# Second product of an expert mixture: six matmuls per visit to an accumulator instead of three

## The chip, the core and the metric

The kernel runs on one core of a Trainium2 chip. The metric is device microseconds (us) of one execution. TensorE (PE) multiplies, with a weight loader of its own (PEld); VectorE (DVE), ScalarE (ACT) and GpSimd (POOL) do the elementwise work; SyncE (SP) issues most DMAs.

## The reference, cut to what matters

A gated linear attention gives 3072 rows of 384. A first mixture, `(a * b @ w3) @ w_out`, maps them to 3072 x 384 again, and a second mixture of four experts follows:

```
p = domain_probs / domain_probs.sum(-1)
out = 0
for e in range(4):
    h = relu(x @ w1[e])              # 3072 x 384 by 384 x 1024
    out += p[:, e:e+1] * (h @ w2[e]) # 3072 x 1024 by 1024 x 384
```

The change is in this last loop alone.

## The kernel before

Every fp32 product is made of three matmuls on operands split in a high and a low part (`mm3`: high by high, low by high, high by low; lines L86, L87 and L88). I call these three matmuls a **visit**. All visits here have 128x128 weights and 384 moving columns.

The second mixture runs in 32 **passes**, numbered 0 to 31: four experts `e`, by four tiles `t` of 768 tokens, by two halves `k` of the 1024 columns of the hidden layer. An even pass has k = 0, an odd one k = 1.

**First product.** A pass forms `x @ w1[e]` for 512 hidden columns and 768 tokens by a scheme with 20 products where plain tiling has 24. The table `PARTS` lists them in 19 **groups**, 0 to 18. A group is one visit (group 10 has two) to one of two PSUM banks of the pool `pho` (the tile is called hps), followed by **steps**, which add or subtract the bank to or from slots of `raw_x`. So the first visit of group g+2 must wait until the last step of group g that reads the bank is over. The steps are numbered 0 to 27 in `PARTS`; steps 0 to 2 are copies on ACT (L1292), the rest additions on DVE (L1294). Steps 6, 15, 17 and 23 read `raw_x` alone; the others read a bank. Some of what the following text needs: group 12 has steps 16 and 17, group 13 step 18, group 14 steps 19 and 20, group 15 steps 21, 22 and 23, group 16 step 24, group 17 steps 25 and 26, group 18 step 27.

**h tiles.** Eight entries "h" of `PARTS` (at groups 6, 8, 10, 11, 14, 15, 17 and 18) turn a finished slot into an **h tile**, a block f of 128 hidden columns for one half of the 768 tokens: two ACT operations, L1275 for the high part and L1276, then one POOL operation for the low part, L1277. Before the change nine buffers are given out in turn.

**Second product.** `h @ w2[e]` has six PSUM accumulators per token tile (the tile is called ops), m = 0 to 5, one for each 128 tokens: m = 0 to 2 for the first half, 3 to 5 for the second. Each takes eight visits: four blocks f in the even pass, four in the odd. The function `second` makes one visit. The visits of a pass are done during the next pass: `blocks` lists the 24 of them, and after each group g the table `SHARE[g]` says how many of them follow. All instructions keep this order on their engine; nothing reorders them. Before the change the list goes h tile by h tile, as they were made, three accumulators for each.

When an accumulator has had its eighth visit, `second` puts one **eviction** on DVE (L1244 for the first expert, L1246 for the others): scale by the expert's share and add to the running sum `ac`, which is then stored. The eighth visits come in the even passes.

In the six passes 7, 8, 15, 16, 23 and 24 DVE also makes the low parts of the next expert's first weights (L1024, behind the steps of groups 3, 5, 7 and 9).

Of the kernel before, what the change touches and what calls it, by code (L numbers as in the profile page):

```python
# [26 lines left out]
HT = 384  # L27
# [42 lines left out]
W_STEPS = ((0, 0, 6), (0, 6, 12), (1, 0, 6), (0, 12, 16), (1, 6, 12), (0, 16, 20), (1, 12, 16), (1, 16, 20))  # L70
SHARE = (2, 1, 1, 1, 0, 1, 2, 1, 1, 1, 1, 1, 1, 1, 1, 2, 2, 2, 2)
SIGN = {"+": ALU.add, "-": ALU.subtract}
# [405 lines left out]
def gated_attention_moe_kernel(tc, qT, kT, aT, vP, w1, w2, w3T, wo, probs, ew, out):  # L478
# [4 lines left out]
    with tc.manual_schedule(), root:  # L483
# [491 lines left out]
        def x_open():  # L975
            for _ in range(4):
                x = wtile([128, 4, 2, HT], F32R, "xo")
                xslots.extend(x[:, n] for n in range(4))
            w = xtp.tile([128, 4 * NP * TT], F32R, tag="xt", name="wa")
            wslots.append(w[:, :2 * NW * 128].rearrange("p (s n c) -> p s n c", s=2, n=NW))  # L980

        def x_sum(eng, t, dst, x, y, op):
# [237 lines left out]
        made = [(f, h) for _, steps in PARTS for _, f, h, op in steps if op == "h"]  # L1220
        turned = [made[2], made[0], made[1]] + made[3:]
        accs = {}
        h_at = {}
        done_h = [0]
        last_use = {o: g for g, (parts, _) in enumerate(PARTS) for _, o in parts}

        def second(i, f, m):
            e, t, k = octs[i]
            half = m // 3
            mine = [b for b, h in (made if k or not i else turned) if h == half]  # L1230
            if (e, t, m) not in accs:
# [4 lines left out]
            last = k == KO - 1 and f == mine[-1]  # L1236
            mm3(nc, ps, hh[:, 0, tok], hh[:, 1, tok], w[:, 0], w[:, 1], k == 0 and f == mine[0], last)
            if not last:
                return
# [16 lines left out]
        def blocks(i):  # L1256
            k = octs[i][2]
            return [(i, f, 3 * h + m) for f, h in (made if k or not i else turned) for m in range(3)]

# [7 lines left out]
        def combine(i, ps, steps, where, left):  # L1267

            for v, x, y, op in steps:
                if op == "h":  # L1270
                    free.append(where.pop(v))
                    s = tmp[:, free[-1]]
                    hh = h_at[i, x, y] = hslots[done_h[0] % len(hslots)]
                    done_h[0] += 1
                    A.activation(out=hh[:, 0], in_=s, func=ACTF.Relu)  # L1275
# [21 lines left out]
        for i, (e, t, k) in enumerate(octs):  # L1297
# [4 lines left out]
            for g, (parts, steps) in enumerate(PARTS):  # L1302
# [7 lines left out]
                combine(i, ps, steps, where, left)  # L1310
                for _ in range(SHARE[g] if i > 1 else g != 4 if i else g > 12):
                    if todo:
                        second(*todo.pop(0))
# [82 lines left out]
```

## Time and profile before

| | |
|---|---|
| median of 3 runs | 1196.36 us (1196.05 to 1198.81) |
| profiled execution, its own time | 1197.35 us |
| its span, first to last instruction | 1195.5 us |
| PE busy | 1167.1 us, 98% |
| DVE busy | 829.2 us, 69% |
| ACT busy | 627.4 us, 52% |
| POOL busy | 445.1 us, 37% |
| passes 0 to 31 | from 440.1 us to 1189.6 us of the span |

The rows of the timeline give a start, a duration, the engine, the line, the tile written, an arrow and the tiles read; in brackets stands idle time of the engine just before, and what ended it. Rows with x2 or more merge neighbours: their time runs from the first start to the last end. DVE and PE are pipelined, so a row may start before the one ahead of it has ended. A matmul lasts 0.34 us in the record, but the next starts some 0.175 us after it.

### The profile page before, as it was taken

How to read it: one execution, taken by the hardware profiler on the slowest of the kernel's cores; microseconds unless marked ns; L12 is line 12 of the kernel's file. 1: busy time of each engine (PE TensorE's matmuls, PEld its weight loads, DVE VectorE, ACT ScalarE, POOL GpSimd, SP SyncE). 2: the span in 40 equal slices, each digit the busy share in tenths (PEclk: the TensorE clock that was granted, in tenths of full speed). 3: DMA queues.
4: the chain of work that ended last, by engine and by line, in shares of the span. 5: the costliest groups of instructions: out<-in, count | busy, mean ns of one | idle time of the engine just before them, and what ended most of it. 6: DMA issues, size and time to landing. Idle time of an engine off the chain costs nothing.

```text
span 1195.5 us, 24960 instructions
## 1 busy us (share of the span) xinstructions
PE 1167.1 (98%) x9186; PEld 1149.3 (96%) x9186; DVE 829.2 (69%) x1513; ACT 627.4 (52%) x1238; POOL 445.1 (37%) x517
## 2 busy tenths in 40 slices
PE   5899999999999999999999999999999999999997
PEld 4799999999999999999999999999999999999997
DVE  8898788966665856667677656667666587576563
ACT  4565555554544445454666655666565545444432
POOL 2133321010000006776744434744433655433332
PEclk9899999999999999999999999999999999999999
DMA  8756675555775696478576595695784863753821
GB/s 318 223 171 188 211 216 200 173 166 192 272 284 177 243 337 226 168 304 292 208 288 225 199 330 203 244 347 178 275 303 156 307 244 127 290 176 142 291 81 43
DMA packets 131171, 269.54 MB, mean 225 GB/s; under 512 B 17376, under 2 KB 64992, under 8 KB 131040
## 3 DMA queue, kind: packets, MB, share of 16 engines
q1 hardware_dynamic: 130176, 266.67, 63.8%
q8 instruction: 75, 1.23, 0.4%
q10 hardware_dynamic: 864, 1.18, 0.3%
q14 instruction: 56, 0.46, 0.1%
HBM read 207.24 MB, written 58.20 MB: 222 GB/s over the span
## 4 chain that ended last, share of the span: by engine, by line
PE 95%; DVE 3%; DMA 1%; issue 0%; POOL 0%; SPq 0%; ACT 0%; DVEq 0%; POOLq 0%
PE ops L87 11%; PE ops L86 11%; PE ops L88 11%; PE hps L86 9%; PE hps L87 9%; PE hps L88 9%; PE abps L86 6%; PE abps L87 6%; PE abps L88 6%; PE xps L86 3%; PE xps L88 3%; PE xps L87 3%; PE yps L673 2%; PE yps L691 1%; PE wps L86 1%; PE wps L88 1%
## 5 line engine op out<-in xcount | busy, mean ns | idle before, releaser
L1294 DVE TENSOR_TENSOR raw_x<-hps,raw_x 128x384 f32<-128x384 f32 x416 | 226.4, 554 | 212.3 <-PE hps L88 197.2
L1277 POOL TENSOR_TENSOR ht<-raw_x,ht 128x384 fp32r<-128x384 f32 x227 | 238.1, 1051 | 274.5 <-ACT raw_x L1276 222.2
L1275 ACT ACTIVATE ht<-raw_x 128x384 fp32r<-128x384 f32 x227 | 118.6, 523 | 228.3 <-DVE raw_x L1294 215.9
L87 PE MATMUL ops<-wb,ht 128*128 128x384 f32 x681 | 231.5, 340 | 0.0
L86 PE MATMUL ops<-wb,ht 128*128 128x384 f32 x681 | 230.8, 339 | 0.0
L88 PE MATMUL ops<-wb,ht 128*128 128x384 f32 x681 | 230.6, 339 | 0.0
L86 PE MATMUL hps<-xo,wa 128*128 128x384 f32 x640 | 217.8, 340 | 2.5 <-DVE raw_x L1294 1.2
L87 PE MATMUL hps<-xo,wa 128*128 128x384 f32 x640 | 215.5, 337 | 0.0
L88 PE MATMUL hps<-xo,wa 128*128 128x384 f32 x640 | 215.1, 336 | 0.0
L1294 DVE TENSOR_TENSOR raw_x<-raw_x,hps 128x384 f32<-128x384 f32 x256 | 136.5, 549 | 25.5 <-PE hps L88 25.1
L1276 ACT ACTIVATE raw_x<-raw_x 128x384 f32<-128x384 f32 x256 | 134.7, 526 | 8.1
L86 PEld LDWEIGHTS hps<-xo,wa 128*128 128x128 f32 x640 | 120.2, 188 | 8.4 <-DVE raw_x L1294 6.0
L86 PEld LDWEIGHTS ops<-wb,ht 128*128 128x128 f32 x681 | 128.0, 188 | 0.0
L88 PEld LDWEIGHTS ops<-wb,ht 128*128 128x128 f32 x681 | 127.9, 188 | 0.0
L87 PEld LDWEIGHTS ops<-wb,ht 128*128 128x128 f32 x681 | 127.5, 187 | 0.0
L87 PEld LDWEIGHTS hps<-xo,wa 128*128 128x128 f32 x640 | 120.2, 188 | 0.0
L88 PEld LDWEIGHTS hps<-xo,wa 128*128 128x128 f32 x640 | 120.1, 188 | 0.0
L1294 DVE TENSOR_TENSOR raw_x<-raw_x 128x384 f32<-128x384 f32 x128 | 88.6, 692 | 4.4
L698 POOL MEMSET Z<- 128x1 f32 x18 | 1.8, 98 | 191.7 <-PE yps L673 191.7
L1277 POOL TENSOR_TENSOR ho<-raw_x,ho 128x384 fp32r<-128x384 f32 x29 | 30.7, 1060 | 105.0 <-DMA xo<-kept 71.4
L86 PE MATMUL abps<-xt,w2h 128*128 128x384 f32 x192 | 66.0, 344 | 0.0
L86 PE MATMUL abps<-xt,w1h 128*128 128x384 f32 x192 | 65.9, 343 | 0.0
(136 smaller groups left out, 2224.2 us busy)
## 6 DMA issues: line engine op xcount, KB each, us to landing
xo<-kept SPq DMA_DIRECT2D x272, 384.0 KB, 6.4
kept<-ac SPq DMA_DIRECT2D x45, 384.0 KB, 2.9
partial<-ac SPq DMA_DIRECT2D x72, 192.0 KB, 1.9
ac<-partial SPq DMA_DIRECT2D x72, 192.0 KB, 6.4
spilled<-g_sb SPq DMA_DIRECT2D x64, 192.0 KB, 2.3
gg<-spilled SPq DMA_DIRECT2D x64, 192.0 KB, 3.3
c_raw<-in_w3T_dram SPq DMA_DIRECT2D x16, 512.0 KB, 4.1
raw_x<-in_w3T_dram SPq DMA_DIRECT2D x8, 1024.0 KB, 7.0
```

Of the source, the lines that this page charges most:

```text
L86: nc.tensor.matmul(out=ps, lhsT=lh, rhs=rh, start=first, stop=False)
L87: nc.tensor.matmul(out=ps, lhsT=ll, rhs=rh, start=False, stop=False)
L88: nc.tensor.matmul(out=ps, lhsT=lh, rhs=rl, start=False, stop=last)
L673: PE.matmul(out=r["y"][rows, p, t], lhsT=Z[rows, p], rhs=r["q"][rows, p, half], start=p == 0, stop=False)
L691: PE.matmul(out=r["y"][rows, p, t], lhsT=v[half, p, g], rhs=r["s"][half, g, p], start=first and t == 0 and p == 0, stop=p == NP - 1)
L698: G.memset(r["Zh"][:, NP - 1, 63:], 0.0)
L1275: A.activation(out=hh[:, 0], in_=s, func=ACTF.Relu)
L1276: A.activation(out=s, in_=s, func=ACTF.Relu)
L1277: G.tensor_tensor(out=hh[:, 1], in0=s, in1=f32(hh[:, 0]), op=ALU.subtract)
L1294: V.tensor_tensor(out=tmp[:, s], in0=ins[0], in1=ins[1], op=SIGN[op])
```

## The change

- `blocks` gives the 24 visits by **pairs**: the first two blocks f of the first half, the first two of the second half, then the last two of each. Within a pair, for each of the three accumulators both blocks follow each other, so that six matmuls in a row go to one accumulator.
- `SHARE` has only 0 and 2, so the visits stand in twos; groups 0, 2, 4, 6, 9, 10 and 13 have none. Passes 0 and 1 get numbers of their own in the same manner.
- The order of blocks is the same in even and odd passes (`turned` is gone).
- A tenth h tile comes from the unused end of the tile `xt` that holds first weights (in order's rows it has the name wa). Buffers are no longer given out in turn: `second` puts one back in the list when its third visit is issued.

```diff
--- before.py
+++ after.py
@@ -68,7 +68,7 @@
     (5, 3, 5, "-"), (5, 12, 0, "x"), (1, 13, 0, "x"), (7, 7, 3, "-"), (7, 14, 0, "x"), (8, 8, 6, "-"),
     (8, 15, 0, "x"), (2, 2, 6, "+"), (2, 16, 0, "x"))
 W_STEPS = ((0, 0, 6), (0, 6, 12), (1, 0, 6), (0, 12, 16), (1, 6, 12), (0, 16, 20), (1, 12, 16), (1, 16, 20))
-SHARE = (2, 1, 1, 1, 0, 1, 2, 1, 1, 1, 1, 1, 1, 1, 1, 2, 2, 2, 2)
+SHARE = (0, 2, 0, 2, 0, 2, 0, 2, 2, 0, 0, 2, 2, 0, 2, 2, 2, 2, 2)
 SIGN = {"+": ALU.add, "-": ALU.subtract}
 NW, NX, NT = 20, 17, 9
 
@@ -978,6 +978,7 @@
                 xslots.extend(x[:, n] for n in range(4))
             w = xtp.tile([128, 4 * NP * TT], F32R, tag="xt", name="wa")
             wslots.append(w[:, :2 * NW * 128].rearrange("p (s n c) -> p s n c", s=2, n=NW))
+            hslots.append(w[:, 2 * NW * 128:2 * NW * 128 + 2 * HT].rearrange("p (s n) -> p s n", s=2))
 
         def x_sum(eng, t, dst, x, y, op):
             r = raw_x[t % 2]
@@ -1218,16 +1219,16 @@
             job(split_b(e, 1), *((i0 + 1, g) for g in range(3, 11)))
 
         made = [(f, h) for _, steps in PARTS for _, f, h, op in steps if op == "h"]
-        turned = [made[2], made[0], made[1]] + made[3:]
+        by_half = [[b for b in made if b[1] == h] for h in range(2)]
+        pairs = [by_half[h][n:n + 2] for n in (0, 2) for h in range(2)]
         accs = {}
         h_at = {}
-        done_h = [0]
         last_use = {o: g for g, (parts, _) in enumerate(PARTS) for _, o in parts}
 
         def second(i, f, m):
             e, t, k = octs[i]
             half = m // 3
-            mine = [b for b, h in (made if k or not i else turned) if h == half]
+            mine = [b for b, _ in by_half[half]]
             if (e, t, m) not in accs:
                 accs[e, t, m] = poo.tile([128, 512], F32, tag="o", name="ops")[:, :DM]
             ps = accs[e, t, m]
@@ -1235,6 +1236,8 @@
             tok = slice(m % 3 * 128, (m % 3 + 1) * 128)
             last = k == KO - 1 and f == mine[-1]
             mm3(nc, ps, hh[:, 0, tok], hh[:, 1, tok], w[:, 0], w[:, 1], k == 0 and f == mine[0], last)
+            if m % 3 == 2:
+                hslots.append(h_at.pop((i, f, half)))
             if not last:
                 return
             b, c = chunks[t * 6 + m]
@@ -1254,8 +1257,7 @@
             nc.sync.dma_start(out=f32(tiles["ac"][:, m // 2, m % 2]), in_=partial[b * NCH + c])
 
         def blocks(i):
-            k = octs[i][2]
-            return [(i, f, 3 * h + m) for f, h in (made if k or not i else turned) for m in range(3)]
+            return [(i, f, 3 * h + m) for pair in pairs for m in range(3) for f, h in pair]
 
         uses = {}
         for _, steps in PARTS:
@@ -1270,8 +1272,7 @@
                 if op == "h":
                     free.append(where.pop(v))
                     s = tmp[:, free[-1]]
-                    hh = h_at[i, x, y] = hslots[done_h[0] % len(hslots)]
-                    done_h[0] += 1
+                    hh = h_at[i, x, y] = hslots.pop(0)
                     A.activation(out=hh[:, 0], in_=s, func=ACTF.Relu)
                     A.activation(out=s, in_=s, func=ACTF.Relu)
                     G.tensor_tensor(out=hh[:, 1], in0=s, in1=f32(hh[:, 0]), op=ALU.subtract)
@@ -1308,7 +1309,7 @@
                     if k == KO - 1 and last_use[o] == g and n + 1 < E * NT2:
                         x_load((t + 1) % NT2, o)
                 combine(i, ps, steps, where, left)
-                for _ in range(SHARE[g] if i > 1 else g != 4 if i else g > 12):
+                for _ in range(SHARE[g] if i > 1 else 2 * (g % 2 == 0 and g < 18) if i else 2 * (g in (13, 15, 17))):
                     if todo:
                         second(*todo.pop(0))
                 for gen in jobs.pop((i, g), ()):
```

What stands in a row, at two places. The first is PE at the start of pass 13, an odd pass, with hps the banks of the first product and ops the accumulators; the number is that of the tile. Before:

```order
L86 MATMUL hps_8911<-xo_5298,wa_5732 128x384
L87 MATMUL hps_8911<-xo_5298,wa_5732 128x384
L88 MATMUL hps_8911<-xo_5298,wa_5732 128x384
L86 MATMUL ops_8917<-wb_7890,ht_5892 128x384
L87 MATMUL ops_8917<-wb_7890,ht_5892 128x384
L88 MATMUL ops_8917<-wb_7890,ht_5892 128x384
L86 MATMUL ops_8921<-wb_7890,ht_5892 128x384
L87 MATMUL ops_8921<-wb_7890,ht_5892 128x384
L88 MATMUL ops_8921<-wb_7890,ht_5892 128x384
L86 MATMUL hps_8926<-xo_5728,wa_5732 128x384
L87 MATMUL hps_8926<-xo_5728,wa_5732 128x384
L88 MATMUL hps_8926<-xo_5728,wa_5732 128x384
```

After:

```order
L86 MATMUL hps_8911<-xo_5298,wa_5732 128x384
L87 MATMUL hps_8911<-xo_5298,wa_5732 128x384
L88 MATMUL hps_8911<-xo_5298,wa_5732 128x384
L86 MATMUL hps_8918<-xo_5728,wa_5732 128x384
L87 MATMUL hps_8918<-xo_5728,wa_5732 128x384
L88 MATMUL hps_8918<-xo_5728,wa_5732 128x384
L86 MATMUL ops_8924<-wb_7889,ht_5891 128x384
L87 MATMUL ops_8924<-wb_7889,ht_5891 128x384
L88 MATMUL ops_8924<-wb_7889,ht_5891 128x384
L86 MATMUL ops_8924<-wb_7743,ht_5891 128x384
L87 MATMUL ops_8924<-wb_7743,ht_5891 128x384
L88 MATMUL ops_8924<-wb_7743,ht_5891 128x384
```

The visit of group 1 (the second hps) stood behind two visits to accumulators; it now follows that of group 0, and the two visits behind it go to one accumulator.

The second place is DVE in pass 12, an even pass, from step 18 (before) and from the first eviction (after); ac marks the evictions. Before:

```order
L1294 TENSOR_TENSOR raw_x_3840<-hps,raw_x_3840 128x384 x2
L1294 TENSOR_TENSOR raw_x_3840<-raw_x_3840,hps 128x384
L1294 TENSOR_TENSOR raw_x_3840<-hps,raw_x_3840 128x384 x2
L1294 TENSOR_TENSOR raw_x_3840<-raw_x_3840 128x384
L1294 TENSOR_TENSOR raw_x_3840<-hps,raw_x_3840 128x384
L1246 SCALAR_TENSOR_TENSOR ac<-ops,p_sb,ac 128x384 x2
L1294 TENSOR_TENSOR raw_x_3840<-hps,raw_x_3840 128x384
L1294 TENSOR_TENSOR raw_x_3840<-raw_x_3840,hps 128x384
L1246 SCALAR_TENSOR_TENSOR ac<-ops,p_sb,ac 128x384 x2
L1294 TENSOR_TENSOR raw_x_3840<-hps,raw_x_3840 128x384
L1246 SCALAR_TENSOR_TENSOR ac<-ops,p_sb,ac 128x384 x2
```

After:

```order
L1249 SCALAR_TENSOR_TENSOR ac<-ops,p_sb,ac 128x384
L1295 TENSOR_TENSOR raw_x_3840<-hps,raw_x_3840 128x384 x2
L1295 TENSOR_TENSOR raw_x_3840<-raw_x_3840,hps 128x384
L1249 SCALAR_TENSOR_TENSOR ac<-ops,p_sb,ac 128x384
L1295 TENSOR_TENSOR raw_x_3840<-hps,raw_x_3840 128x384 x2
L1295 TENSOR_TENSOR raw_x_3840<-raw_x_3840 128x384
L1249 SCALAR_TENSOR_TENSOR ac<-ops,p_sb,ac 128x384
L1295 TENSOR_TENSOR raw_x_3840<-hps,raw_x_3840 128x384
L1249 SCALAR_TENSOR_TENSOR ac<-ops,p_sb,ac 128x384
L1295 TENSOR_TENSOR raw_x_3840<-hps,raw_x_3840 128x384
L1295 TENSOR_TENSOR raw_x_3840<-raw_x_3840,hps 128x384
L1249 SCALAR_TENSOR_TENSOR ac<-ops,p_sb,ac 128x384
L1295 TENSOR_TENSOR raw_x_3840<-hps,raw_x_3840 128x384
```

The six evictions stood in twos behind steps 24, 26 and 27. Now one stands ahead of step 18, one each between 20 and 21 and between 23 and 24, one ahead of and one behind steps 25 and 26, and the sixth behind step 27.

## Rows read from the trace of the kernel before

**Rows 1.** Busy by stretch, passes 0 to 31: each engine's us, PEclk, DMA, GB/s
```profile
440.00:1195.50 755.50, 746.98 (x4226) 740.75 (x4226) 496.81 (x922) 399.48 (x746) 378.97 (x428) 1.00 0.63 228
```

**Rows 2.** Waits of PEld, 440 to 1195: us in total, times, longest
```profile
PEld hps L86 <- DVE raw_x L1294: 6.0, 16, 1.6
```

**Rows 3.** The same waits in 595 to 627, then in 782 to 814
```profile
PEld hps L86 <- DVE raw_x L1294: 1.2, 4, 0.3
...
PEld hps L86 <- DVE raw_x L1294: 1.1, 4, 0.3
```

**Rows 4.** Timeline of PE around one of these waits, pass 7, group 8
```profile
601.36 0.34 PE L88 MATMUL ops<-wb,ht 128*128 128x384 f32 x1
601.66 0.45 PE L86 MATMUL hps<-xo,wa 128*128 128x384 f32 x1
601.95 0.34 PE L87 MATMUL hps<-xo,wa 128*128 128x384 f32 x1
```

**Rows 5.** Timeline of DVE ahead of it: weights, then three steps
```profile
599.73 0.95 DVE L1024 TENSOR_TENSOR wa<-araw,wa 128x768 fp32r<-128x768 f32 x1
600.60 1.48 DVE L1294 TENSOR_TENSOR raw_x<-raw_x,hps 128x384 f32<-128x384 f32 x3
```

**Rows 6.** Timeline of PE: pass 12 starts, group 10 ends, pass 13 starts
```profile
709.28 0.34 PE L86 MATMUL hps<-xo,wa 128*128 128x384 f32 x1
...
721.22 0.33 PE L88 MATMUL hps<-xo,wa 128*128 128x384 f32 x1
...
732.48 0.34 PE L86 MATMUL hps<-xo,wa 128*128 128x384 f32 x1
```

**Rows 7.** DVE, pass 12: steps 12; 17; 18, 19; 20; 23; 26; evictions; 27
```profile
721.65 0.56 DVE L1294 TENSOR_TENSOR raw_x<-hps,raw_x 128x384 f32<-128x384 f32 x1 [1.07 <-PE hps L88]
...
724.30 1.11 DVE L1294 TENSOR_TENSOR raw_x<-raw_x 128x384 f32<-128x384 f32 x1
725.33 1.24 DVE L1294 TENSOR_TENSOR raw_x<-hps,raw_x 128x384 f32<-128x384 f32 x2
726.49 0.54 DVE L1294 TENSOR_TENSOR raw_x<-raw_x,hps 128x384 f32<-128x384 f32 x1
...
728.00 0.56 DVE L1294 TENSOR_TENSOR raw_x<-raw_x 128x384 f32<-128x384 f32 x1
...
730.51 0.55 DVE L1294 TENSOR_TENSOR raw_x<-raw_x,hps 128x384 f32<-128x384 f32 x1
730.97 1.14 DVE L1246 SCALAR_TENSOR_TENSOR ac<-ops,p_sb,ac 128x384 f32<-128x384 f32 x2
732.02 0.55 DVE L1294 TENSOR_TENSOR raw_x<-hps,raw_x 128x384 f32<-128x384 f32 x1
```

**Rows 8.** POOL, pass 12: low parts of the h tiles of steps 13 and 20
```profile
723.98 1.02 POOL L1277 TENSOR_TENSOR ht<-raw_x,ht 128x384 fp32r<-128x384 f32 x1 [2.19 <-ACT raw_x L1276]
...
728.36 1.08 POOL L1277 TENSOR_TENSOR ht<-raw_x,ht 128x384 fp32r<-128x384 f32 x1 [2.08 <-ACT raw_x L1276]
```

**Rows 9.** PE, first matmuls of visits: first mixture; last pass; first mixture again
```profile
256.86 0.34 PE L86 MATMUL xps<-gg,w3h 128*128 128x384 f32 x1
...
273.81 0.34 PE L86 MATMUL xps<-gg,w3h 128*128 128x384 f32 x1
...
1177.67 0.34 PE L86 MATMUL ops<-wb,ht 128*128 128x384 f32 x1
...
1187.74 0.34 PE L86 MATMUL ops<-wb,ht 128*128 128x384 f32 x1
...
282.28 0.34 PE L86 MATMUL xps<-gg,w3h 128*128 128x384 f32 x1
...
288.52 0.34 PE L86 MATMUL xps<-gg,w3h 128*128 128x384 f32 x1
```

**Rows 10.** The end: the six last evictions, and the issues of their stores
```profile
1186.35 3.27 DVE L1246 SCALAR_TENSOR_TENSOR ac<-ops,p_sb,ac 128x384 f32<-128x384 f32 x6 [10.57 <-PE ops L88]
...
1187.00 3.93 ACTq L1250 DMA_DIRECT2D out_dram<-ac  x6
```

## The prediction

> **What bounds the kernel now.** I read the busy times by stretch first. In the passes of the second mixture PE works 746.98 of 755.50 us at full granted clock, 1.00 [rows 1]. The count of matmuls does not change, so only two things can move the time: the distance from one matmul to the next, and PE's waits. The distance is even: pass 12 starts at 709.28 and pass 13 at 732.48 [rows 6], 23.20 us for 44 visits, 0.527 us each or 0.176 us a matmul. Then come the waits: only visits of the first product wait for DVE, 16 times and 6.0 us in all [rows 2], and no visit to an accumulator is in the list. So DVE's queue near such a wait is the next view, and what it collides with on POOL [rows 7, 8]. The end of the program is the third place.
>
> **Matmuls.** 384 changes of accumulator go. What one costs: in the first mixture 32 visits go 24 matmuls to a bank and take 273.81 - 256.86 = 16.95 us, 0.530 each; in the last pass 19 visits, each to another bank, take 1187.74 - 1177.67 = 10.07 us, 0.530 each [rows 9]. I take nothing for them. The Trainium skill ("TensorE: Matmul & The Clock Gate", section on psum-queue depth-cycling) says that cycling through PSUM banks can make TensorE idle briefly between groups, so that its clock falls. By that rule fewer changes would raise the clock; here it reads 1.00 already, so the sum would gain nothing by it either.
>
> **Waits that go.** In six passes DVE also makes weights. PE then waits twice in a pass for a bank, at groups 6 and 8: four times in two passes, 1.2 and 1.1 us of waits in the first two such stretches [rows 3]; the third reads like the first. What one costs PE: the distances 601.36 to 601.66 and to 601.95 are 0.30 and 0.29 instead of 0.176 [rows 4], 0.24 together, of which 0.11 is the slow first matmul after a wait. Twelve make 2.9 us. DVE was 0.95 us on weights just ahead, and three steps followed without a gap [rows 5]. Between groups 4 and 6 there now lie three visits instead of two, 0.53 us more than the 0.12 us that was missing: that wait goes. Between groups 6 and 8 there are three instead of four, so the other may stay: the saving lies between 6 x 0.24 = 1.4 and 2.9 us. I take 1.4, since DVE has the same work there.
>
> **A wait that comes.** I follow DVE through the even pass 12, with durations from its rows. From the end of a product to its step is 0.26 us (matmul at 721.22 [rows 6], plus 0.176; step 12 at 721.65 [rows 7]), and this is never what comes last below.
> - Step 17 reads `raw_x` alone. It began at 724.30 while POOL worked from 723.98 to 725.00 [rows 8], and ended at 725.41, 0.41 after POOL; step 18 began at 725.33 [rows 7]. After the change group 10 has one visit less ahead of it, so steps 12 to 17 and POOL's tile are all 0.53 us earlier. An eviction stands behind step 17 (0.53: two took 730.97 to 732.02 [rows 7]). Both cancel: step 18 is at 725.33 again, step 20 at 726.49.
> - From step 20 to step 23 it was 1.51 us (726.49 to 728.00). An eviction now stands between: step 23 begins at 728.53.
> - POOL's work on the h tile of step 20 stays at 728.36 [rows 8]. It began 0.36 us behind step 23; now it is 0.17 us ahead. Step 23, too, reads `raw_x` alone, so it waits as step 17 did: POOL takes 1.02 us to 729.38, step 23 ends at 729.79, and the next begins 0.08 before that, at 729.71.
> - Behind it are queued: eviction 729.71, step 24 at 730.24, eviction 730.71 (0.47 a step: three in 1.48 [rows 5]), step 25 at 731.24, step 26 at 731.71, eviction 732.17 (0.46 after it, as 730.51 to 730.97), step 27 at 732.70, over at 733.25. Before it began at 732.02 [rows 7].
> - Who waits: step 27 frees the bank for group 1 of pass 13. That visit used to have two visits to accumulators ahead of it; now it is next to group 0 and due at 732.48 + 0.53 = 733.01. PE resumes 0.04 us after a step's end (601.07 + 0.55 against 601.66 [rows 4, 5]), at 733.29: a wait of 0.28, with the slow matmul 0.11 about 0.39 us.
>
> There are 15 even passes with evictions (2 to 30). In pass 22 PE already waits, for the single matmul of the check of the inputs behind group 14; that lets DVE catch up. So 14 x 0.39 = 5.5 us. From both sides: if step 23 is only a little late, DVE is 0.37 us in hand and the cost is 0; with every link 0.05 us longer it is 0.45 x 15 = 6.8.
>
> How POOL and DVE collide matters here. Step 17's row shows a step that stands still until POOL is done. If the two shared at half speed instead, step 23 would end near 729.51 (0.85 us at half speed, then 0.13), the whole queue 0.28 earlier, and the wait would vanish. The Trainium skill ("SBUF — State Buffer", Who interferes with whom) calls it an exclusive lock on a shared port, held for a whole instruction by whichever starts first. The trace agrees (0.41 us after POOL's end), and by that rule the 0.17 us of lead decide.
>
> **Other edits.** Visits to accumulators wait for h tiles on nobody: every tile is made at least 13 groups before its first visit. The tenth buffer and the list take waits off ACT and POOL, which are not late; nothing. Stores follow evictions on SP's queue, now earlier in the pass; loads behind them have a pass of room; nothing. Passes 0 and 1 keep 6 and 18 visits, and DVE there sets when PE goes on: nothing, or 0.3 either way.
>
> **The end.** The last six evictions were done in one row to 1186.35 + 3.27 = 1189.62, and the six stores' issues reached 1187.00 + 3.93 = 1190.93 [rows 10], because evictions 0.53 apart outran issues of up to 0.65. Now an accumulator ends every 1.06 us, so only one issue is left behind the last eviction: its end moves to 1190.27 or earlier. That is 0.7 us. The rows do not show what the end of the span hangs on, so 0 to 0.9.
>
> **Sum.** Against the profiled execution (1197.35, span 1195.5): +5.5 - 1.4 - 0.7 = +3.4 us. That execution is 1.0 us above the median 1196.36; put on the median it gives 1199.8. Own range of this case: 0.25 x 14 - 2.9 - 0.9 = -0.3 to 6.8 - 1.4 = +5.4, 1196.1 to 1201.8. A change under 0.3% (3.6 us: 1192.8 to 1199.9) can't be told from none.
>
> **Rivals.**
> - *The new wait does not come.* If step 23 gets in ahead of POOL, step 27 is over by 732.4 and group 1 starts on time. For it: the margin is 0.17 us out of a chain of some ten links. Against it: times repeat closely from pass to pass in this stage, and POOL's lead comes from step 20 alone. It leaves -1.4 - 0.7 = -2.1, or -3.8 with the second wait gone: 1192.6 to 1194.3, the other side of my forecast. Chance 24%.
> - *More places open.* In the same chain step 24 ends at 730.79 and the visit of group 18 needs its bank at 730.89 (41 visits after 709.28): 0.1 us in hand; group 11 follows group 9 after two visits; ACT's copies for groups 0 to 2 stand behind the late step 27. In passes 2 to 6, 13, 14, 21 and 22 POOL has more work and more steps stand still. One more wait of 0.15 us in 30 passes adds 4.5 us to my sum: 1204. Chance 13%.
> - *The second visit of a pair runs faster.* The first mixture has stretches at 0.520 us a visit (282.28 to 288.52 is twelve visits [rows 9]) beside those at 0.530, with the same code. If the visits in pairs to one accumulator fell into that pace, 12 x 32 x 0.010 = 3.8 us would go: 1196.0 with the new wait, 1190.4 without. Nothing in the rows ties the pace to the bank. Chance 9%.
>
> **Chances.** My case has 54%: slower by over 0.3% in 23, within in 31. First rival: within 16, faster 8. Second: slower 13. Third: within 4, faster 5. So faster 13%, same 51%, slower 36%. The range runs from 1192.5 (some 9% below it, in the first and third rival) to 1203.8 (some 7% above it, in the second).
>
> **What would show it.** Right: in passes 12, 14 and so on step 23 takes over 1.1 us instead of 0.56 and starts just behind POOL; PE waits at group 1 of odd passes, on step 27; pairs of passes take 46.8 us instead of 46.40; the waits at group 6 of the six passes are gone; the last issue ends about 1 us nearer to the last matmul. Wrong: step 23 stays at 0.56, or the odd passes start on time, or the distance of matmuls inside a pair differs from 0.176 us: then the sum fails at that term.

## The result, and the profile after

The changed kernel takes 1207.34 us (median of 5 runs, 1206.26 to 1208.77) against 1196.36 us (5 runs, 1194.46 to 1198.81). The ratio is 1.0086, with a 95% interval of 1.0072 to 1.0101: it is slower by 0.7 to 1.0%. I forecast 1199.8 us, slower by 0.3%, and a range that ended at 1203.8; the sign was right and the size was not. Most of the 11 us are waits of PE: one kind that I had forecast (4.0 us), one that I had overlooked (3.0), and several in the first passes (4.0).

The profiled execution has a span of 1207.0 us, 11.4 us more than before. From the first matmul of pass 0 to the last one of the program it is 758.63 us instead of 748.53, which is 10.1 of the 11.4; 1.0 us lies behind the last matmul and 0.3 us ahead of pass 0, in code that the change does not touch.

From pass 0 to just behind the last matmul, by windows (microseconds, then busy time and count of PE, PEld, DVE, ACT and POOL, then PEclk, DMA share, GB/s; [rows 1] runs on to the end of the span, which adds 0.7 us of DVE):

```profile
440.40:1199.40 759.00, 752.65 (x4226) 738.81 (x4226) 516.92 (x921) 399.04 (x745) 378.48 (x428) 1.00 0.63 226
```

The matmuls are the same 4226 and the clock is 1.00 again. ACT and POOL work as long as before. DVE works some 20 us longer with the same instructions. Two groups of the list by line say which of them grew (behind the first bar stand busy time and mean ns of one; before, the first group read 88.6, 692 and the second 40.8, 611):

```profile
L1295 DVE TENSOR_TENSOR raw_x<-raw_x 128x384 f32<-128x384 f32 x128 | 105.1, 821 | 4.4
...
L1249 DVE SCALAR_TENSOR_TENSOR ac<-ops,p_sb,ac 128x384 f32<-128x384 f32 x72 | 43.8, 608 | 10.9 <-PE ops L88 10.9
```

One eviction takes what it did (its total rose by 3 us only because neighbours overlap less). The steps that read `raw_x` alone, which are 6, 15, 17 and 23, went from 692 to 821 ns on average: they stand still more often. What PE feels of it is in the waits of PEld, the answer to [rows 2]:

```profile
PEld hps L86 <- DVE raw_x L1295: 14.8, 37, 1.0
PEld hps L86 <- ACT raw_x L1293: 2.8, 4, 1.6
```

From 16 waits of 6.0 us to 37 of 14.8, and a second line that was 0.2 us before: waits for ACT's copies, steps 0 to 2.

To place them I took the distance between the starts of all neighbouring matmuls of the passes (the two small ones of the check of the inputs left out). Where it is over some 0.2 us, I summed what it has over 0.1755 us, the usual distance. This **excess** holds the wait and the slow first matmul after it. It is 6.3 us before and 16.6 us after:

| where | before | after | forecast of the difference | measured |
|---|---|---|---|---|
| group 1 of odd passes | 0 | 4.0 | +5.5 | +4.0 |
| the six weight passes | 2.8 | 4.5 | -1.4 | +1.7 |
| passes 0 to 6, without group 1 of 3 and 5 | 2.6 | 6.6 | 0 (passes 0 and 1: either way 0.3) | +4.0 |
| all the rest of the passes (20 and 22 above all) | 1.0 | 1.6 | 0 | +0.6 |
| behind the last matmul's start | 6.9 | 7.9 | -0.7 | +1.0 |

The distance itself did not move: its mean without waits is 175.75 ns before and 175.72 ns after.

**The wait that was forecast** is there, link by link. DVE in pass 12 of the changed kernel, which starts at 715.31: steps 20, eviction of m 1, steps 21 and 22, step 23, and, behind the left-out rows, step 27. Then POOL's h tile, then PE at the start of pass 13:

```profile
732.51 0.54 DVE L1295 TENSOR_TENSOR raw_x<-raw_x,hps 128x384 f32<-128x384 f32 x1
732.97 0.61 DVE L1249 SCALAR_TENSOR_TENSOR ac<-ops,p_sb,ac 128x384 f32<-128x384 f32 x1
733.50 1.01 DVE L1295 TENSOR_TENSOR raw_x<-hps,raw_x 128x384 f32<-128x384 f32 x2
734.55 1.26 DVE L1295 TENSOR_TENSOR raw_x<-raw_x 128x384 f32<-128x384 f32 x1
...
738.69 0.55 DVE L1295 TENSOR_TENSOR raw_x<-hps,raw_x 128x384 f32<-128x384 f32 x1
...
734.36 1.02 POOL L1278 TENSOR_TENSOR ht<-raw_x,ht 128x384 fp32r<-128x384 f32 x1 [2.58 <-ACT raw_x L1277]
...
738.89 0.34 PE L88 MATMUL hps<-xo,wa 128*128 128x384 f32 x1
739.29 0.45 PE L86 MATMUL hps<-xo,wa 128*128 128x384 f32 x1
739.58 0.34 PE L87 MATMUL hps<-xo,wa 128*128 128x384 f32 x1
```

Step 23 began 0.19 us behind POOL and ended at 735.81, 0.43 us after POOL's end at 735.38. Step 27 ended at 739.24, and PE went on at 739.29. The distances 0.40 and 0.29 are 0.34 us too long together; 0.39 were forecast.

**A wait that was not forecast** stands in the weight passes, at group 12. In pass 7 of the changed kernel, DVE makes the fourth low part of the weights and then the two steps that read the bank of group 10 (the second row and the first half of the third); POOL's h tile of the same time and PE at group 12 follow:

```profile
608.53 1.36 DVE L1025 TENSOR_TENSOR wa<-araw,wa 128x512 fp32r<-128x512 f32 x1
609.82 0.55 DVE L1295 TENSOR_TENSOR raw_x<-hps,raw_x 128x384 f32<-128x384 f32 x1
610.28 1.00 DVE L1295 TENSOR_TENSOR raw_x<-raw_x,hps 128x384 f32<-128x384 f32 x2
...
608.33 1.02 POOL L1278 TENSOR_TENSOR ht<-raw_x,ht 128x384 fp32r<-128x384 f32 x1 [0.51 <-ACT raw_x L1277]
...
610.30 0.34 PE L88 MATMUL ops<-wb,ho 128*128 128x384 f32 x1
610.88 0.45 PE L86 MATMUL hps<-xo,wa 128*128 128x384 f32 x1 [0.24 <-DVE raw_x L1295]
```

The weight instruction reads two operands from SBUF (`araw` and `wa`), as step 23 does, and it, too, stood still until POOL was done. In the kernel before the same instruction ran 0.32 us ahead of POOL's, took its 0.68 us, and POOL was the one to wait (1.25 us, and 1.02 when it runs alone):

```profile
604.02 0.68 DVE L1024 TENSOR_TENSOR wa<-araw,wa 128x512 fp32r<-128x512 f32 x1
...
604.34 1.25 POOL L1277 TENSOR_TENSOR ht<-raw_x,ht 128x384 fp32r<-128x384 f32 x1 [0.52 <-ACT raw_x L1276]
```

The order of the two turned because of the places. POOL's tile hangs on the product of group 8, the weight part stands behind the step of group 9. Between these two groups there now lie two visits instead of one (1.69 us from start to start in pass 7, and 1.16 before), so POOL gained 0.53 us on the weight part: 0.32 us behind became 0.20 ahead. All six weight passes show it, with leads of 0.19 to 0.21 us.

**The early passes** have the largest single wait, in pass 3 at group 3. In passes 2 to 4 ACT and POOL also prepare the last token tile (L988 on ACT, L985 and L991 on POOL). One of ACT's copies for the banks stands in its queue behind such an instruction, which waits for POOL. ACT, POOL, then PE:

```profile
503.18 0.47 ACT L1293 ACTIVATE raw_x<-hps 128x384 f32<-128x384 f32 x1
504.87 0.52 ACT L988 ACTIVATE stage<-raw_x 128x384 fp32r<-128x384 f32 x1 [1.22 <-POOL raw_x L985]
505.30 0.85 ACT L1293 ACTIVATE raw_x<-hps 128x384 f32<-128x384 f32 x2
...
503.83 1.01 POOL L985 TENSOR_TENSOR raw_x<-raw_x 128x384 f32<-128x384 f32 x1
...
504.21 0.34 PE L88 MATMUL hps<-xo,wa 128*128 128x384 f32 x1
505.83 0.44 PE L86 MATMUL hps<-xo,wa 128*128 128x384 f32 x1 [1.28 <-ACT raw_x L1293]
```

### The profile page after: what moved, and what is told of

It reads as the page before. It is cut to its first block, busy times and chain, and to the rows that moved or that the text cites. A ratio compares the mean times of both kernels' runs of the same rounds, so it can differ in the third digit from the quotient of the medians.

```text
span 1207.0 us, 24990 instructions
## 1 busy us (share of the span) xinstructions
PE 1172.6 (97%) x9186; PEld 1147.3 (95%) x9186; DVE 850.6 (70%) x1513; ACT 627.4 (52%) x1238; POOL 444.2 (37%) x517
## 3 DMA queue, kind: packets, MB, share of 16 engines
q8 instruction: 75, 1.23, 0.4%
## 4 chain that ended last, share of the span: by engine, by line
PE 80%; DVE 11%; issue 5%; POOL 1%; DMA 1%; ACT 0%; SPq 0%; DVEq 0%; POOLq 0%; ACTq 0%
PE ops L86 9%; PE ops L87 8%; PE ops L88 8%; PE hps L86 8%; DVE raw_x L1295 7%; PE hps L87 7%; PE hps L88 7%; PE abps L86 6%; PE abps L87 6%; PE abps L88 5%; PE xps L86 3%; PE xps L87 3%; PE xps L88 3%; DVE ac L1249 2%; PE yps L673 2%
## 5 line engine op out<-in xcount | busy, mean ns | idle before, releaser
L1278 POOL TENSOR_TENSOR ht<-raw_x,ht 128x384 fp32r<-128x384 f32 x206 | 215.3, 1048 | 253.0 <-ACT raw_x L1277 217.3
L1276 ACT ACTIVATE ht<-raw_x 128x384 fp32r<-128x384 f32 x206 | 108.0, 524 | 214.7 <-DVE raw_x L1295 203.2
L86 PE MATMUL ops<-wb,ht 128*128 128x384 f32 x618 | 210.1, 340 | 0.0
L88 PE MATMUL ops<-wb,ht 128*128 128x384 f32 x618 | 209.8, 340 | 0.0
L87 PE MATMUL ops<-wb,ht 128*128 128x384 f32 x618 | 209.6, 339 | 0.0
L1295 DVE TENSOR_TENSOR raw_x<-raw_x,hps 128x384 f32<-128x384 f32 x256 | 132.3, 548 | 43.0 <-PE hps L88 43.0
L86 PEld LDWEIGHTS hps<-xo,wa 128*128 128x128 f32 x640 | 120.1, 188 | 19.9 <-DVE raw_x L1295 14.8
L86 PEld LDWEIGHTS ops<-wb,ht 128*128 128x128 f32 x618 | 116.1, 188 | 0.0
L88 PEld LDWEIGHTS ops<-wb,ht 128*128 128x128 f32 x618 | 116.1, 188 | 0.0
L87 PEld LDWEIGHTS ops<-wb,ht 128*128 128x128 f32 x618 | 115.8, 187 | 0.0
L1295 DVE TENSOR_TENSOR raw_x<-raw_x 128x384 f32<-128x384 f32 x128 | 105.1, 821 | 4.4
L1278 POOL TENSOR_TENSOR ho<-raw_x,ho 128x384 fp32r<-128x384 f32 x25 | 26.8, 1071 | 112.7 <-DMA xo<-kept 71.4
L86 PE MATMUL xps<-gg,w3h 128*128 128x384 f32 x192 | 65.4, 340 | 1.2 <-ACT raw_x L838 1.2
```

Source lines behind the costliest of these rows:

```text
L86: nc.tensor.matmul(out=ps, lhsT=lh, rhs=rh, start=first, stop=False)
L87: nc.tensor.matmul(out=ps, lhsT=ll, rhs=rh, start=False, stop=False)
L88: nc.tensor.matmul(out=ps, lhsT=lh, rhs=rl, start=False, stop=last)
L1278: G.tensor_tensor(out=hh[:, 1], in0=s, in1=f32(hh[:, 0]), op=ALU.subtract)
L1295: V.tensor_tensor(out=tmp[:, s], in0=ins[0], in1=ins[1], op=SIGN[op])
```

## The experiments

The question is which of the change's parts costs what: the new places of the visits (`SHARE`), the order by pairs, the evictions that this order moves, or the tenth tile. The runs' times scatter by some 3 us to either side of a median (at most 4, but for one run of the kernel before, 7 us above it), a part of it ahead of pass 0, which starts anywhere from 438.0 to 441.3 us in these profiles. So the table gives beside the median the passes of the profiled execution (first to last matmul start) and their excess.

| kernel | median, us | ratio to before, 95% interval | passes, us | excess, us |
|---|---|---|---|---|
| before | 1196.36 | | 748.53 | 6.3 |
| after | 1207.34 | 1.0086 (1.0072 to 1.0101) | 758.63 | 16.6 |
| e7_before_tenth | 1197.47 | 0.9997 (0.9983 to 1.0011) | 748.74 | 6.6 |
| e1_share_back | 1206.02 | 1.0061 (1.0039 to 1.0082) | 757.54 | 15.6 |
| e2_order_back | 1203.22 | 1.0040 (1.0024 to 1.0057) | 754.59 | 12.4 |
| e9_pairs_evict_back | 1197.49 | 1.0008 (0.9999 to 1.0017) | 749.02 | 6.7 |
| e3_evict_later | 1202.10 | 1.0034 (1.0022 to 1.0046) | 752.54 | 10.4 |
| e5_pool_halves | 1200.24 | 1.0027 (1.0011 to 1.0043) | 751.95 | 9.9 |
| e4_weight_later | 1204.36 | 1.0057 (1.0037 to 1.0078) | 755.87 | 13.7 |
| e6_early_share | 1205.50 | 1.0068 (1.0047 to 1.0089) | 755.72 | 13.5 |
| e12_three_repairs | 1195.56 | 0.9997 (0.9987 to 1.0006) | 748.09 | 6.0 |
| e8_before_weight | 1195.76 | 0.9989 (0.9976 to 1.0003) | 748.38 | 6.2 |
| e10_before_halves | 1197.63 | 1.0005 (0.9995 to 1.0014) | 749.43 | 7.1 |
| e11_halves_weight | 1198.01 | 1.0014 (1.0005 to 1.0024) | 749.45 | 7.2 |

The kernel before was timed again beside each set: 1197.98 us with e1 to e4, 1197.14 with e5 to e8, 1196.14 with e9 to e12. The ratios are against these.

Read by excess against the 6.3 us of the kernel before, the tenth tile alone is +0.3 (e7). With that tile in all of them, the order by pairs is +0.4 (e9), the new places are +6.1 (e2), and the order with its evictions spread over the pass is +9.3 (e1). All together are +10.3, so the parts do not add up: the places also decide at which groups the spread evictions are felt.

### The tenth h tile alone

```diff
-                    hh = h_at[i, x, y] = hslots[done_h[0] % len(hslots)]
-                    done_h[0] += 1
+                    hh = h_at[i, x, y] = hslots.pop(0)
```

together with the new buffer and the line that returns one to the list, in the kernel before.

> The kernel before with the tenth h tile alone, given out as tiles come free; order and places of the visits as before. The prediction took nothing for it: no change within 0.1%, and the same waits of PE as before. Rival (the tile takes waits off ACT and POOL that PE felt, or adds some): a change of over 0.1% of 1196.4, 1.2 us.

No change, 0.9997, and the same excess by pass but in pass 22 (1.3 instead of 0.9 us). In this kernel the tile is free.

### Places of the visits as before, order by pairs kept

```diff
-SHARE = (0, 2, 0, 2, 0, 2, 0, 2, 2, 0, 0, 2, 2, 0, 2, 2, 2, 2, 2)
+SHARE = (2, 1, 1, 1, 0, 1, 2, 1, 1, 1, 1, 1, 1, 1, 1, 2, 2, 2, 2)
...
-                for _ in range(SHARE[g] if i > 1 else 2 * (g % 2 == 0 and g < 18) if i else 2 * (g in (13, 15, 17))):
+                for _ in range(SHARE[g] if i > 1 else g != 4 if i else g > 12):
```

> The changed kernel with the visits given out as in the kernel before (its row of numbers, and its rule for passes 0 and 1); the order by pairs of blocks and the tenth h tile stay. Theory A (the waits come from where visits now lie, none behind groups 0, 2, 4, 6, 9, 10 and 13): two visits stand behind group 0 again, so the late step 27 hurts nobody and the wait at group 1 of odd passes goes (12 x 0.33 = 4 us); the waits at group 12 of the six weight passes turn back into the old ones at groups 6 and 8 (4.6 to 2.8 us); the losses of passes 1 to 6 (4.7 us) go. Time 1196.5 to 1200, its upper part if step 24 is now too late for group 18. Theory B (the order by pairs, with evictions between the steps of an even pass, costs the time wherever the visits lie): 1205 to 1208.

My theory A fell: 1206.02, within the range of theory B. The waits at group 1 of odd passes are gone and those of the weight passes are the old ones, as it said; but 15.6 us of excess are left. Now every even pass from 8 on waits at group 15 (0.43 us) and group 18 (about 0.13). DVE in pass 12, then PE at group 15:

```profile
728.05 0.60 DVE L1249 SCALAR_TENSOR_TENSOR ac<-ops,p_sb,ac 128x384 f32<-128x384 f32 x1
728.57 1.23 DVE L1295 TENSOR_TENSOR raw_x<-hps,raw_x 128x384 f32<-128x384 f32 x2
...
728.67 0.34 PE L88 MATMUL ops<-wb,ht 128*128 128x384 f32 x1
729.17 0.44 PE L86 MATMUL hps<-xo,wa 128*128 128x384 f32 x1 [0.16 <-DVE raw_x L1295]
```

An eviction, 0.52 us of the queue, stands ahead of step 18, which has the bank for group 15. In the kernel before the first eviction of a pass comes behind group 16. So I formed another theory: neither the order nor the places cost anything by themselves; the evictions that the order by pairs brings between the steps do, and the places decide only which group meets it. What this says of the order was borne out (e9 below); what it says of the places was not, as the next run shows.

### Order of the visits as before, new places kept

```diff
-            return [(i, f, 3 * h + m) for pair in pairs for m in range(3) for f, h in pair]
+            return [(i, f, 3 * h + m) for f, h in (made if octs[i][2] or not i else turned) for m in range(3)]
```

with `turned` and `mine` as in the kernel before.

> The changed kernel with its new row of numbers, but the accumulator visits in the order of the kernel before (three visits of one f block, then the next block), so that all six evictions stand behind groups 16, 17 and 18. Theory A1 (step 23 meets POOL because an eviction stands between steps 20 and 23): step 23 takes 0.56 us again and the wait at group 1 of odd passes goes although no visit lies behind group 0; the waits at group 12 of the weight passes and the losses of passes 1 to 6 stay: 1207.3 - 4.0 = 1203.3, within 1202 to 1204.5. Rival (no visit behind group 0 is enough to make PE wait): 1206.5 to 1208.

1203.22, on the mark by luck: the waits at group 1 lost 1.9 us and not 4.0, and the rest of the gain came where I had not counted on it (0.8 us in pass 22, 1.0 in passes 0 to 6, 0.5 in the weight passes). With the evictions back behind groups 16 to 18, no wait at group 1 is left in passes 5, 9, 11, 17, 25 and 29; five odd passes keep one of 0.35 us (13, 19, 21, 27, 31), and pass 3 one of 0.26.

These six show what decides. In the pass ahead of each of them POOL began 0.10 to 0.20 us before step 23, which then took 1.23 to 1.33 us. In passes 4, 6, 8, 10, 16, 24 and 28 POOL began 0.01 to 0.32 us behind step 23, which took 0.56 us, and PE did not wait at the next group 1. (In passes 14 and 22 POOL's tile had been under way for 0.9 and 0.6 us; no wait followed.) Pass 10, which starts at 665.56, and pass 12, which starts at 711.96, have step 23 at the same place, 18.63 us behind their start; of each pass DVE's step 23, then POOL:

```profile
684.19 0.56 DVE L1296 TENSOR_TENSOR raw_x<-raw_x 128x384 f32<-128x384 f32 x1
684.44 1.20 POOL L1279 TENSOR_TENSOR ht<-raw_x,ht 128x384 fp32r<-128x384 f32 x1 [2.40 <-ACT raw_x L1278]
...
730.59 1.33 DVE L1296 TENSOR_TENSOR raw_x<-raw_x 128x384 f32<-128x384 f32 x1
730.49 1.02 POOL L1279 TENSOR_TENSOR ht<-raw_x,ht 128x384 fp32r<-128x384 f32 x1 [2.04 <-PE ops L87]
```

Why POOL comes now ahead and now behind no run tells. The new places make it matter: in pass 10 step 27 ends 0.44 us before group 1 of pass 11 starts, where the kernel before had 1.50 us in hand in pass 12, and the collision takes 0.64. The waits at group 12 of the weight passes (3.2 us) and passes 1 to 3 stay: these come from the places.

### Order by pairs, places and evictions as before

e1_share_back, with the evictions put aside and issued two each behind groups 16, 17 and 18:

```diff
+                for _ in range(2 if g > 15 and later else 0):
+                    evict(*later.pop(0))
```

> Like e1_share_back (order by pairs and tenth tile, visits given out as in the kernel before), and the six evictions of an even pass are issued where the kernel before has them: two each behind groups 16, 17 and 18. Only the order of the visits themselves and the h tiles differ from before. Theory (a visit costs the same in any order; the evictions between DVE's steps made e1 slow): PE's waits in the passes fall from 15.6 us in e1 to about the 6.3 us of before, 1196 to 1198. Rival (the order by pairs has a price of its own, by later release of h tiles or by the tiles that it reads): 1201 or more, with waits of PE for h tiles or at groups 15 and 18 still there.

1197.49, and an excess of 6.7 us: the 8.9 us that e1 had beyond it are gone with the evictions' places alone. PE's waits for DVE are nearly those of [rows 2]:

```profile
PEld hps L86 <- DVE raw_x L1304: 6.3, 17, 1.6
```

So the order of the visits by itself costs nothing that can be measured. Only six of the twelve pairs of a pass stand in a row here; in the changed kernel all twelve do, and the matmuls' distance there (175.72 against 175.75 ns) says that six matmuls in a row to one accumulator take as long as two times three.

### One eviction moved

```diff
+            if m == 1 and (e, t) != octs[-1][:2]:
+                later.append((e, t, m, ps))
+            else:
+                evict(e, t, m, ps)
...
+                while g == 15 and later:
+                    evict(*later.pop())
```

> The changed kernel with one eviction moved: that of accumulator 1 is issued behind the steps of group 15 and no longer between steps 20 and 23. The order of matmuls is untouched. The theory of the prediction: step 23 begins 0.53 us earlier, ahead of POOL, takes 0.56 instead of 1.26 us, step 27 is over about 0.7 us earlier and the waits at group 1 of odd passes go: 12 x 0.33 = 4.0 us, 1203.3. Rival (the sum of DVE's work decides, not its place): the eviction only moves, step 27 ends as late as before, 1207.

1202.10, and the excess is 6.2 us less; 4.0 were forecast. In pass 12 (from 712.89) step 23 is ahead of POOL and takes 0.56 us, and no odd pass has a wait at group 1. DVE's step 23 and the two evictions behind it, then POOL, which now waits for DVE:

```profile
731.60 0.56 DVE L1304 TENSOR_TENSOR raw_x<-raw_x 128x384 f32<-128x384 f32 x1
732.08 1.14 DVE L1258 SCALAR_TENSOR_TENSOR ac<-ops,p_sb,ac 128x384 f32<-128x384 f32 x2
...
731.94 1.10 POOL L1287 TENSOR_TENSOR ht<-raw_x,ht 128x384 fp32r<-128x384 f32 x1 [2.58 <-ACT raw_x L1286]
```

The rest of the gain, 2.2 us, was not expected: 0.85 us in pass 3 at group 3, 0.5 in pass 22, 0.85 at group 18 of four passes and at group 8 of pass 20. I did not follow how the eviction reaches these; the last lies ahead of all evictions of its pass.

### POOL's h tile in two instructions

```diff
-                    G.tensor_tensor(out=hh[:, 1], in0=s, in1=f32(hh[:, 0]), op=ALU.subtract)
+                    for c in (slice(0, HT // 2), slice(HT // 2, HT)):
+                        G.tensor_tensor(out=hh[:, 1, c], in0=s[:, c], in1=f32(hh[:, 0, c]), op=ALU.subtract)
```

> The changed kernel with POOL's low part of each h tile written by two instructions of 192 columns instead of one of 384. Theory of a lock held by one instruction at a time: step 23 gets in between the halves and ends about 0.4 us after the first one, near +20.0 us of the even pass instead of +20.49; the whole queue behind it is 0.4 to 0.5 us earlier, and the wait at group 1 of odd passes (0.33 us each) goes or falls below 0.1: 1203 to 1204.5. Rival (the two engines share the port at a slower pace, or POOL's next instruction always goes first): step 23 ends where it did or later, the time stays at 1207 or above it by what the extra POOL instructions cost.

1200.24, more than hoped. Nothing of DVE's or PE's order changed, yet all waits at group 1 went, and those at group 12 fell from 0.50 to 0.16 us. Step 23 of pass 12 (which starts at 711.84), then POOL's two halves:

```profile
730.65 0.83 DVE L1296 TENSOR_TENSOR raw_x<-raw_x 128x384 f32<-128x384 f32 x1
...
730.47 1.48 POOL L1279 TENSOR_TENSOR ht<-raw_x,ht 128x192 fp32r<-128x192 f32 x2 [1.87 <-PE ops L88]
```

The row of POOL holds both halves. The first takes 0.61 us, to 731.08; step 23 ends at 731.48, 0.40 after it, and the second half takes 0.92 us instead of 0.60, since now POOL waits. So DVE gets in between two instructions of POOL, and in these rows the two do not share while one of them runs. The Trainium skill ("SBUF — State Buffer", Who interferes with whom) says that a DVE instruction with two SBUF inputs contends with a POOL instruction that reads SBUF, that this is an exclusive lock on a shared pair of ports, and that a DVE instruction with one SBUF input, outside its two-port modes, does not contend. The trace agrees: with the 0.40 and 0.92 us above for the lock, and with the steps that read one operand from a bank, which took 0.54 to 0.56 us whether POOL worked beside them or not.

### The fourth weight part one group later

```diff
-                        *((i0 - 1 + k, g) for g in (1, 2, 3, 4, 5, 6, 7, 9)))
+                        *((i0 - 1 + k, g) for g in (1, 2, 3, 4, 5, 6, 7, 10)))
```

> The changed kernel with the fourth low part of the weights for the next expert issued behind the steps of group 10 instead of group 9, in the passes 7, 8, 15, 16, 23 and 24. If that DVE instruction, kept waiting by POOL, is what makes PE wait at group 12: these six waits of 0.50 us go, 3.0 us, 1204.3, with nothing new at group 13, ahead of which lie four visits. Rival (DVE is behind there whatever the place): the wait moves to group 13 and the time stays at 1206.5 to 1208.

1204.36. All six waits at group 12 are gone (3.0 us), and nothing came at group 13. Behind group 10 the instruction meets no h tile and takes 0.69 us:

```profile
608.52 0.69 DVE L1025 TENSOR_TENSOR wa<-araw,wa 128x512 fp32r<-128x512 f32 x1
```

### Passes 0 to 6 as before

```diff
-                for _ in range(SHARE[g] if i > 1 else 2 * (g % 2 == 0 and g < 18) if i else 2 * (g in (13, 15, 17))):
+                for _ in range(SHARE0[g] if 1 < i < 7 else SHARE[g] if i > 1 else g != 4 if i else g > 12):
```

(`SHARE0` is the row of the kernel before.)

> The changed kernel with the visits of passes 0 to 6 given out as in the kernel before; from pass 7 on nothing changes. If the losses of passes 1 to 6 come from where visits lie (groups without visits behind them while POOL and ACT finish the input of the last tile): passes 1 to 6 lose 0.5 us instead of 5.1 us, 1207.3 - 4.6 = 1202.7, within 1201.5 to 1204. Rival (they come from the order by pairs or the tenth h tile): 1206 to 1208.

1205.50: a miss by 2.8 us. Passes 1 to 6 lose 2.7 us, not the 0.5 that I expected, against 5.1 in the changed kernel. What is left is at group 15 of passes 2, 4 and 6 (0.4 to 0.5 us each) and at group 3 of pass 3 (0.9): the first is the wait of e1_share_back, and e9 shows that both vanish with the evictions' old places. So each of the two makes a part of the early loss, and the parts overlap: with the evictions spread and the old places 2.2 us of the 4.6 stay (this run), with the new places and the old evictions 3.3 (e2), with both old none (e9).

### Three repairs at once

The edits of e3, e4 and e6 together.

> The changed kernel with three repairs at once: the eviction of accumulator 1 behind group 15 (alone -5.2 us), the fourth weight part behind group 10 (alone -3.0), the visits of passes 0 to 6 as in the kernel before (alone -1.8). If the three losses are separate and together are what the change cost, the sum holds: 1207.3 - 10.0 = 1197.3, within 1196 to 1198.5, and PE's waits in the passes come to 5 to 7 us as in the kernel before. Rival (a loss that is none of the three, in the matmuls or at the end of the program): 1199.5 or more.

1195.56 us, ratio 0.9997, and an excess of 6.0 us: the changed order of matmuls runs as fast as the old one. PE's waits for DVE in its passes:

```profile
PEld hps L87 <- DVE raw_x L1305: 5.2, 15, 1.6
```

The three repairs give back what the passes lost, though the gains are not separate (their sum, 6.2 + 2.9 + 3.1 = 12.2 us of excess, is more than the 10.6 that went), since early passes are in two of them. Nor is it the old pattern of waits: group 15 of passes 2, 4 and 6 still loses 1.1 us together, and the weight passes lose 1.6 us less than in the kernel before.

### Versions meant to be faster

The kernel before with the last four weight steps behind groups 6, 7, 8 and 10, with POOL's halves, and with both (the edits are those of e4 and e5 with other numbers).

> The kernel before with the last four of the eight steps of weight making moved: behind groups 6, 7, 8 and 10 instead of 5, 6, 7 and 9, in the passes 7, 8, 15, 16, 23 and 24. If its twelve waits at groups 6 and 8 come from a low part of 0.95 us on DVE ahead of a bank's step: the first goes or moves with the instruction; where two visits and the later groups give more room, up to 2.8 us are gained, 1193.5 to 1195.5. Rival (the wait moves with the instruction): 1196 to 1197.5.

> The kernel before with POOL's low part of each h tile in two instructions of 192 columns. In the changed kernel that was worth 7 us, since DVE stood behind POOL there. In the kernel before the twelve waits of the weight passes come from DVE's own 0.95 us instruction, not from POOL: if that reading is right the halves change little, 1195.5 to 1197. Rival (DVE behind POOL is part of those waits as well): the excess of PE's intervals in the six weight passes falls from 2.8 us to below 1.5 us, 1194 to 1195.5.

> The kernel before with both: POOL's low parts in halves, and the last four weight steps behind groups 6, 7, 8 and 10. Meant as the fastest version. By the profile PE's waits in the passes are 6.3 us before, of which 2.8 us are in the weight passes and 0.9 to 1.3 us at the check of the inputs in pass 22; the moved weight steps alone left 1.9 us of the 2.8. Expected 1194 to 1196; if DVE's own work sets the rest, no different from the moved steps alone, 1195.8.

None beats the kernel before by what can be measured. With the weight steps moved (0.9989, 0.9976 to 1.0003) the wait at group 8 goes, the one at group 6 stays at 0.24 us, and a new one of 0.1 to 0.4 comes at group 15. The halves leave the six weight passes at 0.46 us each, as the reading of [rows 5] said: there DVE is late by its own 0.95 us and not by POOL. They cost 1.0 us in passes 3 and 4 instead, where POOL also prepares the last token tile and has 0.14 us more to do for each h tile. Both together add up to a little slower, against what I expected.

## Why the prediction was wrong

The sum had +3.4 us and the span grew by 11.4. Two steps failed: a lock on the weight parts that was never looked for (3.1 us between forecast and result in the weight passes), and passes 0 to 6, which beside the forecast wait were put at nothing (4.0). The end adds 1.7, passes 20 and 22 0.6, and the one wait that was forecast takes 1.5 back.

- **Matmuls, 0 us: right.** 175.75 and 175.72 ns; e9 has the order by pairs alone at 1.0008 (0.9999 to 1.0017). The rival of a faster second visit is out.
- **The wait that comes, +5.5: right in mechanism, a little too large.** Every link from step 20 to PE came within 0.05 us of the working. It measured 0.33 to 0.35 us instead of 0.39, in ten steady passes; passes 3 and 5 add 0.6. It is missing in pass 23, as forecast, and in passes 7 and 15: in pass 14 step 23 found POOL at other work and took 0.85 us, and in pass 6 it came 0.5 us earlier. 4.0 us in all. That POOL's 0.2 us of lead decide is shown by e3, where it is gone, by e2, where 0.10 us make the wait and passes without that lead have none, and by e5, where POOL holds DVE up for a shorter time. The rival in which the wait does not come is out.
- **Waits that go, -1.4: the first step that failed.** The waits at group 6 went, and those at group 8 fell from 0.23 to 0.14 us: 1.9 us gained, inside my bounds of 1.4 and 2.9. But I closed that part there. I followed the lock of POOL on step 23 and not on the other DVE instruction that reads two operands from SBUF, the weight part. With two visits between groups 8 and 9 the fourth part came 0.2 us behind POOL's tile instead of 0.32 ahead (its rows stand above) and was 0.68 us longer; with one visit less between groups 9 and 12, group 12 waited 0.50 us in each of the six passes: +3.0, and +0.5 at group 18. With some small ones the net is +1.7 instead of -1.4. e4 shows it: with that one instruction moved all six waits go.
- **Other edits, 0 in passes 0 and 1 and nothing said of 2 to 6: the second step that failed**, by 4.0 us. My second rival named the places (passes 2 to 6, the ACT copies) and gave them one wait of 0.15 us in 30 passes. They came in few passes and were large: 1.5 us at one group of pass 3. Pass 1, which was to move by 0.3 us at most, lost 0.9, by the places alone (e1 and e6 have it back at 0.15). The tenth tile costs nothing (e7); that visits wait for h tiles on nobody was wrong once, in pass 0 (0.45 us for the new tile), without a change in the sum of that pass.
- **The end, -0.7: right in its mechanism, not seen in the sum.** The last issue ended at 1194.80 + 5.63 = 1200.43, 1.36 us after the start of the last matmul instead of 2.31 [rows 10]:

```profile
1194.80 5.63 ACTq L1253 DMA_DIRECT2D out_dram<-ac  x6
```

  In e5 the span ends 6.21 us after that start, 0.71 less than the 6.92 before, as forecast. In the changed kernel it ends 7.91 after it: while the program closes, the other engines wait for ScalarE, which answers at 1206.63 and 1.6 us after the last work of any other. Pauses of 1 to 1.8 us at that point are in the profiles of e1 to e4, e6, e9 and e12 too, and not in those of before, e5, e7, e8, e10 and e11. What ScalarE waits for there no run tells; it stays open.
- **The range.** Its upper end added rival 2 to my sum as one mean wait. It had itself named the passes in which POOL has more work. A bound there would have been a whole POOL instruction (1.0 us) in each of a few passes, and not 0.15.

## What to carry to other kernels

When work is put between the steps of an engine that is nearly late, the order of the instructions decides more than their sum: the same six evictions spread over the pass cost 9 us more than behind groups 16 to 18 with the old places of the visits (e1 against e9), and 4 us more with the new ones (the changed kernel against e2). Where two engines lock each other out, list every instruction that takes part in the lock, with its lead over the other engine in us, before and after the change; each lead that changed its sign cost the DVE instruction 0.7 us here (0.56 to 1.26, 0.68 to 1.36), and there were two such places, of which I had checked one. And cutting the longer side of the lock in two is worth trying where its engine has time: it gave 7 us here, and cost 1 us in passes where POOL had other work.

## What the runs showed that I had not expected

- A DVE instruction with two SBUF inputs that found POOL at work on an h tile ended 0.40 to 0.45 us after POOL's end (384 columns, 0.56 us alone) and 0.54 us after it (512 columns of weights, 0.68 alone), so three quarters of its own duration came after POOL's end. The other way round POOL's 1.02 us became 1.08 to 1.25 in the rows shown here, and up to 1.44 where it began just behind DVE (e2).
- POOL's instruction of 384 columns takes 1.02 us, two of 192 take 0.60 each and 1.16 together, since they overlap by a little: 0.14 us for the second instruction, and DVE's instruction gets in between them.
- That cut alone took the changed kernel from 1207.34 to 1200.24 us, with the order of instructions on PE and DVE untouched; in the kernel before, where steps also stand behind POOL (step 17 in [rows 7]) but PE's waits do not hang on it, the same cut gave nothing (1.0005).
